# A fused attention and MLP kernel on one Trainium2 core: one front for two passes, two scales for w_in, and a new order of its tasks

## The chip, the core and the metric

The kernel runs on one NeuronCore of a Trainium2 chip. Five engines work side by side, each through its own list of instructions in a fixed order: TensorE (PE: matrix products and transposes), VectorE (DVE), ScalarE (ACT), GpSimd (POOL) and SyncE (SP), which starts the transfers between the chip's main memory (HBM) and the on-chip memory (SBUF). An engine waits where its next instruction needs a result that isn't there yet; it never takes a later one first. TensorE writes its products into a small memory of its own (PSUM), from where VectorE and ScalarE read them. The metric is the time of one execution in microseconds of the device.

## The reference

Attention for 8 batches of 8 heads, with 576 positions and 64 numbers a head, and then a two-layer MLP over all 4608 tokens. A position sees its own block of 64 and the blocks before it.

```python
scores = np.matmul(q, k.transpose(0, 1, 3, 2)) / np.sqrt(D)
scores = np.where(block_i >= block_j, scores, -1e9)      # blocks of 64 positions
attn = np.exp(scores - scores.max(-1, keepdims=True))
attn = attn / (attn.sum(-1, keepdims=True) + 1e-9)
o = np.matmul(attn, v)                                   # (8, 8, 576, 64)
x = o.transpose(0, 2, 1, 3).reshape(8 * 576, 512)
h = x @ w_in                                             # 512 -> 2048
out = np.square(np.maximum(h, 0.0)) @ w_out              # 2048 -> 512
```

## The kernel before

All numbers are fp32 in and out, but most products run on halves: a number is split into a high and a low f16 (`h`, then `l` from what the high half left over), and a product of two such numbers is three products, high by high, high by low and low by high. So that the halves use f16's range, each operand is first scaled by a power of two that is found from its largest value.

**Attention.** The work is cut into 40 passes, each for one batch and two heads. Passes 0 to 7 are short (the first 192 positions of batches 0 and 1), 8 to 11 do the rest of batch 0 in fp32 turns, and 12 to 39 are turned by DMA and need v in halves. A pass has these tasks, the letter being the name in the planner: `A` scores on TensorE (tile `side`), `B` their maxima on VectorE (`nmx`), `C` exponentials on ScalarE (`p`, with sums `sm`), `S` and `R` the reciprocals of the sums (`rs`), `D`, `H`, `L` the probabilities in halves (`p_rows`), `T` or `E` and `F` the transposition (`p_turned`), `G` the products with v (`px`), `X` their copy to `x`. A pass from 12 on also has a **front**, which finds v's scale: `fv` (ScalarE sums the absolute values of each row into `st`), `fa` (TensorE turns that column into a row, `pm`), `fb` (VectorE takes its largest, `top`), `fc` (TensorE spreads this over 128 partitions), `fd` (VectorE keeps the exponent, `m`), `fe` (three GpSimd steps: `m`, the scale `s`, and `xsc`), `vh` (high half of v, ScalarE) and `vl` (low half, VectorE).

**Norm.** For each of the 12 chunks of 384 tokens, `nq` adds up the squares `sq` of x on TensorE; VectorE makes a factor from it, and `h` and `l` write x in halves into `xt_all`.

**MLP.** The first four chunks are plain: for each of 16 units `ph{chunk}_{f}`, twelve products of 128x384 (`pair<-xt_all,w`), then `pos` and `sqr` (relu and square, tile `r`), `top` (the high half, a CAST into `hidden`) and `rem` (the low half, a subtraction `hidden<-r,hidden`). The other eight chunks save products in the manner of Strassen, with seven half-size products `p1` to `p7` for four units (tile `group`) and additions on ScalarE and VectorE. Behind both, `po` multiplies `hidden` with w_out (`pair<-w,hidden`), `ob` scales the result by the token's factor `uv` (one step on VectorE, two on ScalarE), and `out` stores it.

**Weights.** w_in and w_out come in 16 slices each. Before a slice can be used, its numbers are made whole (`bits` on GpSimd, `prelu` on ScalarE, `join` on VectorE), its largest value is found (`max`), and a chain `w0a` to `w0e` (w_in) or `w1a` to `w1e` (w_out) of VectorE and TensorE steps makes one scale out of all 16; then each slice is cast (`cast`) and its low half made (`low`).

**What sets the order.** A planner in the program (`Plan`) builds the lists of all engines ahead of time. `add(name, queue, ns, after, rank, make, takes, frees)` registers a task with its engine, or with a price for each of several engines, what it waits for, its rank and the buffers that it takes and gives back. `run` goes through an imagined time: it takes the task that can start earliest, among equals the one of the lowest rank, and puts it on the engine where it would end first. `DRAGS` says by what share of a GpSimd task's time VectorE is counted as held up. The ranks come from constants (`W0`, `W1`, `CHAIN`, `CALM`, `FRONT`, `TURN`) and from a table of single corrections, `SHIFTS`:

```python
if q == "POOL" and free["DVE"] > at:
    free["DVE"] += self.drag(name) * queues[q]
```

All instructions are recorded by one helper, so they all stand on one line of the program (L124); they are told apart by their tiles.

Of the kernel before, what the change touches and what calls it, by code (L numbers as in the profile page):

```python
# [19 lines left out]
P = 128  # L20
D = 64
# [12 lines left out]
CALM = 1195.46  # L34
# [19 lines left out]
W0 = (-248.45, 10.9, 139.39, 8.21, 175.27, 11.63, 23.26)  # L54
W1 = (-30.45, -241.86, -561.58, -723.11, -96.62)
NORMS = (-3.68, -3.62)
YR = (90.87, 1.94, 1.28, -9.6)
UR = (225.07, 13.43, 15.26)
LATER = 16
EASE = 61.67  # L60
SPARE = 157.67
SLACK = 0
EARLY = 542.67
BEGIN = 281.87
FILLER = 10000
CHAIN = 488.46
FRONT = 95.73
# [4 lines left out]
TURN = (2121.43, -14.33)  # L72
# [28 lines left out]
A20 32, A21 -9.5, A32 -520, A9 -300, B12 6.4, B14 520, B15 -190, B17 -8.6, B23 -97, B25 130, B27 74, B29 -220, B30 -51, B31 -120, B33 430,  # L101
B35 960, B37 -230, B38 -1100, B4 61, C12 730, C13 690, D6 1200, D7 640, D8 30, E4 870, F8 900, H12 -270, H16 270, H20 390, H21 210, H32 350,
H36 130, L13 76, L17 -240, L18 -440, L19 -780, L26 110, L28 -360, L33 -1500, L34 -590, Q6 740, R12 -930, R13 28, R20 -420, R3 -110, R38
-380, R5 -550, S12 -120, S8 -2200, T15 670, T18 72, T31 -190, X18 -450, X19 250, c226 150, fa12 620, fb12 -1200, fb14 21, fb21 -580, fd14
920, fd19 4.7, fv33 1000, h015 150, h1 98, h2 110, h234 200, h44 -11, h46 -490, h53 -1400, h54 -890, h65 1400, ic0 -460, ic1 -420, l014 51,
l2 290, l233 38, l42 540, l44 -2, l54 7.5, load21 -170, low0 -6, ob0 26, ob7 230, p1 -32, p23 -21, p36 -130, p38 -160, p410 -63, p45 -180,
p47 200, p48 -190, p510 -13, p610 -140, p63 -250, p65 -120, p77 290, p78 -91, po7 1300, pos0 -88, pos1 -820, pos2 420, prelu0 -51, r10 -340,
r11 -190, rem0 -4.5, rem116 -160, rem123 580, rem218 4.2, s15 240, s16 -710, s23 20, s24 84, s26 -58, s32 610, s35 -4.6, sa0 58, sa2 128.6,
sq116 110, sq123 -160, sq126 -130, sq128 210, sq2110 -280, sq223 390, sqr0 1600, t0 240, top1 1200, top4 -390, uv0 -98, vl17 820, vl21 -38,
vl31 110, vl32 710, vl34 -21, vl36 -21  # L110
# [40 lines left out]

class Plan:


    DRAGS = (("bits", 0.4), ("cast", 0.3), ("rem", 0.15), ("D", 0.35), ("top", 0), ("t", 0.4), ("s", 0.2))
    LAG = {"PE": 250, "DVE": 180, "ACT": 220, "POOL": 200, "SP": 100}

    def __init__(self, rings):
        self.tasks, self.rings, self.holders, self.before, self.lands = {}, rings, {}, {}, {}
# [15 lines left out]
    def run(self):  # L175
# [12 lines left out]
        def ready(name):  # L188
# [10 lines left out]
            for q in queues:  # L199
                lag = self.LAG[q] + (MARGIN if q == "PE" and rank >= LATE else 0)  # L200
                at = free[q]
                for n in needs:
                    at = max(at, issued[n] if on[n] == q and n not in self.lands else end[n] + lag)
                cost = at + queues[q] + (EASE + (SPARE if name[0] in "Dc" and "POOL" in queues else 0) if q == "DVE" else 0)
                if best is None or cost < best[0]:
                    best = cost, at, q
            yield best[1], rank, name, best[2]

        while open_:
# [27 lines left out]
            if len(queues) > 1:  # L237
                make(q)
            else:
                make()  # L240
        assert not any(need.values()), [n for n in need if need[n]][:20]
# [3 lines left out]
def attention_moe_kernel(ctx: ExitStack, tc: tile.TileContext, qk1, v1, qk, ks, vm, vt, w_in, w_out, out):  # L245
# [35 lines left out]
    vraw = [const.tile([P, 2, 5, D], F32, name=f"vraw{i}") for i in range(2)]  # L281

# [57 lines left out]
    tokA = const.tile([P, 1], F32, name="tokA")  # L340
    tokB = const.tile([P, 1], F32, name="tokB")
# [62 lines left out]
    wsc = [const.tile([P, 1], F32, name=f"wsc{i}") for i in range(2)]  # L404
# [15 lines left out]
    beyond = []  # L420

# [6 lines left out]
    def weight_scale(wi, m):  # L428

        tok = (tokA, tokB)[wi]  # L430
        if wi:
            nc.vector.tensor_scalar(tok, m, 2.0**-5, None, op0=ALU.mult)
        else:
# [3 lines left out]
        nc.vector.tensor_scalar(  # L437
            wsc[wi].bitcast(I32), tok.bitcast(I32), -1, 254 << 23, op0=ALU.mult, op1=ALU.add
        )
        if wi:  # L440
            nc.vector.tensor_scalar(tokB, tokB, tokA, None, op0=ALU.mult)
        else:
            nc.vector.tensor_scalar(tokA, tokA, 2.0 ** (A_X + A_W - 1), None, op0=ALU.mult)

    def weight_part(wi, f):
# [20 lines left out]
        def summed(o):  # L466
            nc.scalar.activation(raws[wi][f][2], whole, AF.Prelu, scale=2.0**-9, alpha=-1.0, accum_out=o)

        def high(q):
            if q == "ACT":  # L470
                nc.scalar.activation(wh, whole, AF.Copy, scale=wsc[wi])
            else:
                (nc.vector if q == "DVE" else nc.gpsimd).tensor_scalar(wh, whole, wsc[wi], None, op0=ALU.mult)

        def low():
            nc.vector.scalar_tensor_tensor(wl, whole, wsc[wi], wh, op0=ALU.mult, op1=ALU.subtract)
# [45 lines left out]
    def front(t):  # L522


        u, c = t["u"], t["chunks"]
        v32 = t["v32"][:, :, 0:c, :]
        box = {}

        def v_sum():
            box["st"] = small.tile([P, 1], F32, tag="st", name=f"st_{u}")  # L530
            t["v16"] = p2.tile([P, 2, 2, 5, D], F16, tag="v16", name=f"v16_{u}")
            nc.scalar.activation(t["v16"][:, 0, :, 0:c, :], v32, AF.Abs, accum_out=box["st"])

        def turned():
            pm = box["pm"] = ps_x.tile([P, 512], F32, tag="x", name=f"pm_{u}")
            nc.tensor.transpose(pm[:1, :P], box["st"], ident)

        def largest():
            box["top"] = small.tile([1, 1], BF16, tag="top", name=f"top_{u}", bufs=1)
# [1238 lines left out]
```

## Time and profile before

| what | value |
|---|---|
| median of three runs | 989.27 us (988.4 to 989.52) |
| profiled execution | 989.28 us |
| its span in the trace | 987.5 us |
| TensorE busy | 956.1 us of the span (97%), 8027 products |
| VectorE busy | 786.2 us (80%) |
| ScalarE busy | 606.0 us (61%) |
| GpSimd busy | 210.0 us (21%) |

The span goes from the first to the last instruction that the trace holds; what the execution took beyond it lies around it. Busy time counts an engine's own instructions, and a matrix product that runs at half clock counts for as long as it lasts. A row of the timeline groups neighbouring instructions of one kind (x12 is twelve of them), and the bracket at its end is the idle time ahead of it with what ended it: `[1.39 <-DMA first<-in_qk]` is 1.39 us of waiting for a transfer into the tile `first`. In a row of groups the last column is all idle time ahead of the group's instructions, with the releaser of most of it.

### The profile page before, as it was taken

How to read it: one execution, taken by the hardware profiler on the slowest of the kernel's cores; microseconds unless marked ns; L12 is line 12 of the kernel's file. 1: busy time of each engine (PE TensorE's matmuls, PEld its weight loads, DVE VectorE, ACT ScalarE, POOL GpSimd, SP SyncE). 2: the span in 40 equal slices, each digit the busy share in tenths (PEclk: the TensorE clock that was granted, in tenths of full speed). 3: DMA queues.
4: the chain of work that ended last, by engine and by line, in shares of the span. 5: the costliest groups of instructions: out<-in, count | busy, mean ns of one | idle time of the engine just before them, and what ended most of it. 6: DMA issues, size and time to landing. Idle time of an engine off the chain costs nothing.

```text
span 987.5 us, 20889 instructions
## 1 busy us (share of the span) xinstructions
PE 956.1 (97%) x8027; PEld 598.8 (61%) x8027; DVE 786.2 (80%) x1749; ACT 606.0 (61%) x1535; POOL 210.0 (21%) x354
## 2 busy tenths in 40 slices
PE   6789899999999999999999999999999999999998
PEld 5455544554554554596486586596577476496675
DVE  6798998878999669799789698899679788576361
ACT  5799963865887685565465566667566567353240
POOL 3635310002334213132022012122012011101000
PEclk9889989999999999999999999999999999999999
DMA  9835454585753713954760652945561560700001
GB/s 357 308 136 179 116 157 88 127 177 135 153 135 94 153 35 67 206 110 93 148 142 12 133 122 45 211 68 150 132 143 21 136 127 20 137 12 11 23 2 33
DMA packets 221649, 114.92 MB, mean 116 GB/s; under 512 B 195290, under 2 KB 203756, under 8 KB 221548
## 3 DMA queue, kind: packets, MB, share of 16 engines
q1 hardware_dynamic: 221548, 113.57, 48.2%
q8 instruction: 63, 1.03, 0.4%
q14 instruction: 38, 0.31, 0.1%
HBM read 58.21 MB, written 9.46 MB: 69 GB/s over the span
## 4 chain that ended last, share of the span: by engine, by line
PE 68%; DVE 13%; ACT 7%; issue 6%; DMA 3%; POOL 2%; SPq 0%; POOLq 0%; DVEq 0%; ACTq 0%
PE pair L124 33%; PE group L124 21%; PE side L124 6%; PE px L124 5%; DVE w L124 3%; DVE p_rows L124 3%; ACT p L124 2%; DVE nmx L124 2%; PE po L124 2%; ACT r L124 1%; DMA w<-in_w_in 1%; DVE _AluOpType.subtract L124 1%; DVE xt_all L124 1%; DMA hidden<-in_w_in 1%; DVE r L124 1%
## 5 line engine op out<-in xcount | busy, mean ns | idle before, releaser
L124 PE MATMUL pair<-w,hidden 128*128 128x512 f16 (+1 forms) x1680 | 380.2, 376 | 2.1 <-DVE ob L124 1.4
L124 PEld LDWEIGHTS <-hidden 128*128 128x128 f16 x1776 | 167.4, 98 | 185.3 <-issue 14.8
L124 PEld LDWEIGHTS <-w 128*128 128x128 f16 x2304 | 202.2, 98 | 71.6 <-issue 20.7
L124 ACT ACTIVATE p<-side,nmx 128x576 f32<-128x576 f32 (+8 forms) x264 | 139.7, 539 | 87.3 <-DVE nmx L124 73.1
L124 PE MATMUL group<-xt_all,w 128*128 128x192 f16 x1536 | 141.8, 246 | 0.0
L124 DVE SCALAR_TENSOR_TENSOR p_rows<-p,rs,p_rows 128x64 f16<-128x64 f32 (+6 forms) x264 | 138.2, 562 | 4.5 <-DMA p_turned<-p_rows 1.5
L124 PE MATMUL pair<-xt_all,w 128*128 128x384 f16 x768 | 136.3, 334 | 3.4 <-DVE xt_all L124 3.4
L124 DVE TENSOR_REDUCE nmx<-side 128x1 f32<-128x448 f32 (+8 forms) x288 | 123.2, 479 | 12.8 <-PE side L124 12.5
L124 ACT CAST hidden<-r 128x384 f16<-128x384 f32 x188 | 94.8, 510 | 26.4 <-DVE r L124 23.5
L124 POOL TENSOR_SCALAR sm<-sm 128x2 f32<-128x2 f32 (+2 forms) x104 | 29.1, 279 | 381.5 <-ACT p L124 373.3
L124 PE MATMUL group<-xt_all,turned_w 128*128 128x192 f16 x1152 | 108.6, 246 | 0.0
L124 PE MATMUL side<-qk 64*64 64x512 f32 (+2 forms) x480 | 95.2, 492 | 6.7 <-ACT p L124 6.1
L124 ACT ACTIVATE r<-group 128x384 f32<-128x384 f32 x100 | 48.9, 489 | 85.0 <-PE group L124 83.8
L124 PEld LDWEIGHTS <-turned_w 128*128 128x128 f16 x1152 | 95.8, 98 | 7.5 <-issue 2.0
L124 POOL TENSOR_TENSOR hidden<-r,hidden 128x384 f16<-128x384 f32 x55 | 57.9, 1053 | 195.6 <-ACT hidden L124 131.0
L124 DVE TENSOR_TENSOR hidden<-r,hidden 128x384 f16<-128x384 f32 x137 | 81.3, 599 | 16.3 <-ACT hidden L124 15.1
L124 ACT ACTIVATE p_rows<-p,rs 128x128 f16<-128x128 f32 (+9 forms) x148 | 67.6, 501 | 37.8 <-DVE rs L124 34.3
L124 PE MATMUL side<-ks,qk 64*64 64x128 f32 (+4 forms) x576 | 90.6, 420 | 0.0
L124 PE MATMUL px<-p_turned,v 128*64 128x384 f16 (+5 forms) x1168 | 70.9, 270 | 0.5 <-ACT x L124 0.2
L124 PEld LDWEIGHTS <-v 128*64 128x64 f16 x1128 | 50.6, 110 | 27.4 <-issue 16.9
L124 DVE SCALAR_TENSOR_TENSOR r<-group,r 128x384 f32<-128x384 f32 x96 | 52.9, 552 | 14.0 <-PE group L124 10.3
L124 DVE SCALAR_TENSOR_TENSOR r<-r 128x384 f32<-128x384 f32 x98 | 58.8, 603 | 3.6 <-ACT r L124 1.2
(147 smaller groups left out, 1069.3 us busy)
## 6 DMA issues: line engine op xcount, KB each, us to landing
qk<-in_qk SPq DMA_DIRECT2D x32, 576.0 KB
ks<-in_ks SPq DMA_DIRECT2D x32, 320.0 KB
vraw<-in_vm SPq DMA_DIRECT2D x30, 256.0 KB
w<-in_w_out SPq DMA_DIRECT2D x10, 512.0 KB
out<-ob SPq DMA_DIRECT2D x17, 256.0 KB
w<-in_w_in SPq DMA_DIRECT2D x8, 512.0 KB
out<-ob SPq DMA_DIRECT2D x26, 128.0 KB
hidden<-in_w_in SPq DMA_DIRECT2D x6, 512.0 KB
```

The lines of the kernel that those rows point to most:

```text
L124: i = make(*a, **k)
```

## The change

It has three parts.

- **w_in gets two scales**, one for slices 0 to 7 and one for 8 to 15 (`SHARES`). The chain `w0a` to `w0e` becomes two chains (`w0a0` to `w0e0`, `w0a1` to `w0e1`) and a step `w0e` that joins them; the casts of the first eight slices wait for the first chain alone. What was a constant factor (`C_H`) in the steps behind w_in's products becomes a pointer to `rescale`, with a value for each half.
- **A front is done for two passes at once.** The values of v are loaded for both (`vals{i}`, apart from the rows of q and k), `fv` writes two columns of `st`, and `fa` to `fe` run once for both, on two columns. The high half `vh` may go to VectorE, and only it takes a buffer `v16`; `fv` writes its unused result to `unread`.
- **The planner** gets other numbers in `DRAGS`, a table `BIAS` that is added to the price of a kind of task on an engine, more tasks that may go to VectorE (`F`, `X`, `Q`, w_out's `max`), and new constants and `SHIFTS` throughout.

```diff
-    DRAGS = (("bits", 0.4), ("cast", 0.3), ("rem", 0.15), ("D", 0.35), ("top", 0), ("t", 0.4), ("s", 0.2))
+    DRAGS = (("bits", 0.3), ("cast", 0.2), ("rem", 0.42), ("D", 0.25), ("top", 0), ("t", 0.5), ("s", 0.55), ("fe", 0.05))
...
+SHARES = (8, 16)
...
+BIAS = {'D ACT': 677, 'D DVE': -122, 'D POOL': 142, 'F ACT': -1214, 'F DVE': -817, 'H ACT': -44, 'H DVE': -119, 'c ACT': -342, 'c DVE': -40, 'cast ACT': 2073, 'cast DVE': -672, 'cast POOL': 818, 'h ACT': -137, 'h DVE': -231, 'ob ACT': -14706, 'ob DVE': 211, 'rem DVE': 0, 'rem POOL': -5929, 's DVE': 590, 's POOL': 360, 'sq ACT': 728, 'sq DVE': 1129, 't DVE': -13772, 't POOL': 722, 'top ACT': 157, 'top DVE': 249, 'X DVE': 3195, 'Q DVE': -81, 'max DVE': 88, 'vh ACT': 5746, 'Q ACT': -26, 'X ACT': 444, 'max ACT': -1113, 'pos ACT': 179, 'pos DVE': 13, 'vh DVE': -436}
...
-                cost = at + queues[q] + (EASE + (SPARE if name[0] in "Dc" and "POOL" in queues else 0) if q == "DVE" else 0)
+                cost = at + queues[q] + BIAS.get(f"{kind_of(name)} {q}", 0) + (EASE + (SPARE if name[0] in "Dc" and "POOL" in queues else 0) if q == "DVE" else 0)
...
+    def shares_joined():
+
+        nc.vector.reduce_max(tokA, toks, axis=AX.X)
+        nc.vector.tensor_scalar(rescale[:, 0:1].bitcast(I32), tokA.bitcast(I32), -1, 254 << 23, op0=ALU.mult, op1=ALU.add)
+        nc.vector.tensor_scalar(rescale, toks, rescale[:, 0:1], C_H, op0=ALU.mult, op1=ALU.mult)
+        nc.vector.tensor_scalar(tokA, tokA, 2.0 ** (A_X + A_W - 1), None, op0=ALU.mult)
...
-        def v_sum():
-            box["st"] = small.tile([P, 1], F32, tag="st", name=f"st_{u}")
-            t["v16"] = p2.tile([P, 2, 2, 5, D], F16, tag="v16", name=f"v16_{u}")
-            nc.scalar.activation(t["v16"][:, 0, :, 0:c, :], v32, AF.Abs, accum_out=box["st"])
+        def v_sum(e):
+            t = pair[e]
+            if e == 0:
+                box["st"] = small.tile([P, 2], F32, tag="st", name=f"st_{u}")
+            c = t["chunks"]
+            nc.scalar.activation(unread[:, :, 0:c, :], t["v32"][:, :, 0:c, :], AF.Abs, accum_out=box["st"][:, e : e + 1])
 
         def turned():
             pm = box["pm"] = ps_x.tile([P, 512], F32, tag="x", name=f"pm_{u}")
-            nc.tensor.transpose(pm[:1, :P], box["st"], ident)
+            nc.tensor.transpose(pm[:2, :P], box["st"], ident)
 
         def largest():
-            box["top"] = small.tile([1, 1], BF16, tag="top", name=f"top_{u}", bufs=1)
-            nc.vector.tensor_reduce(box["top"], box["pm"][:1, :P], axis=AX.X, op=ALU.max)
+            mx = small.tile([2, 1], F32, tag="top", name=f"mx_{u}", bufs=1)
+            dg = box["dg"] = small.tile([2, 2], BF16, tag="vd", name=f"vd_{u}", bufs=1)
+            nc.vector.tensor_reduce(mx, box["pm"][:2, :P], axis=AX.X, op=ALU.max)
+            nc.vector.tensor_scalar(dg, ident[:2, :2], mx, None, op0=ALU.mult)
 
         def spread():
-            nc.tensor.matmul(box["pm"][:, P : P + 1], ones_bf[:1], box["top"], start=True, stop=True)
+            nc.tensor.matmul(box["pm"][:, P : P + 2], ones_bf[:2], box["dg"], start=True, stop=True)
...
+            if i % 2 == 0:
...
+                if i - 2 >= WHOLE:
+                    prior = [f"vl{i - 2}", f"vl{i - 1}"]
...
+                add(f"vals{i}", "SP", 1900, prior, ahead + 1, both, size=2 * P * 2 * S * 4)
+                for e in range(2):
+                    add(f"fv{i + e}", "ACT", 740, [f"vals{i}"] + [f"fv{i}"] * e, r, go("v_sum", e))
+                add(f"fa{i}", "PE", 120, [f"fv{i}", f"fv{i + 1}"], r, go("turned"), ("x",))
```

The order of the instructions changes on every engine. The first place is TensorE's list at the end of chunk 0, before the change: here `nq` stands behind chunk 0's sixteenth unit, whose last product is the first row. (`_0_3` in a name is pass 12 and `_1_3` pass 13; the last number of a name is its buffer.)

```order
LDWEIGHTS w_104
MATMUL pair_81<-xt_all,w_104 128x384
LDWEIGHTS ones_bf
MATMUL nq_1_1414<-sq_1_0_1149,ones_bf 128x384
LDWEIGHTS ones_bf
MATMUL nq_1_1414<-sq_1_2_1361,ones_bf 128x384
MATMUL pm_1_3_1417<-ident,st_1_3_1386 1x128
MATMUL side_75<-qk_1_3_1008 64x512 x2
...
MATMUL pm_0_3_1441<-top_0_3_1453,ones_bf 128x1
LDWEIGHTS w_104
MATMUL pair_76<-xt_all,w_104 128x384
```

The last row is chunk 1's first product; between `nq` and it there are two transposes of fronts, four groups of scores and one spread. After the change the same stretch reads:

```order
MATMUL nq_1_1374<-sq_1_2_1320,ones_bf 128x384
MATMUL pm_0_3_1377<-ident,st_0_3_1339 2x128
LDWEIGHTS w_105
MATMUL pair_81<-xt_all,w_105 128x384
...
MATMUL side_80<-qk_1_3_956 64x320 x2
MATMUL side_80<-ks_1_3_958,qk_1_3_956 64x256 x2
MATMUL side_75<-qk_1_3_956 64x512 x2
MATMUL side_75<-ks_1_3_958,qk_1_3_956 64x384 x2
...
MATMUL pm_0_3_1377<-vd_0_3_1448,ones_bf 128x2
LDWEIGHTS w_105
MATMUL pair_76<-xt_all,w_105 128x384
```

Now `nq` stands behind the thirteenth unit: the fourteenth unit (twelve products) lies between it and the scores, and the fifteenth and sixteenth (24 products, at the second "...") between the scores and the spread. The fronts of passes 12 and 13 (`_0_3` and `_1_3`) are one transpose of two columns.

The second place is GpSimd's list where the second layer's input of chunk 1 is made, before the change. `sm` are sums of exponentials, `m`, `s` and `xsc` a front.

```order
TENSOR_SCALAR sm_1_3_7_1646<-sm_1_3_7_1646 128x2
TENSOR_SCALAR sm_1_3_4_1825<-sm_1_3_4_1825 128x2
TENSOR_TENSOR hidden<-r_0_1515,hidden 128x384
TENSOR_SCALAR m_2_3_1890<-m_2_3_1890 128x1
TENSOR_SCALAR s_2_3_1900<-m_2_3_1890 128x1
TENSOR_SCALAR xsc_2_3_1902<-m_2_3_1890 128x1
TENSOR_SCALAR sm_2_3_8_1893<-sm_2_3_8_1893 128x2
```

One low half of `hidden` stands between sums and fronts. After the change:

```order
TENSOR_SCALAR sm_1_3_7_1810<-sm_1_3_7_1810 128x2
TENSOR_TENSOR hidden<-r_0_1533,hidden 128x384
TENSOR_TENSOR hidden<-r_1_1554,hidden 128x384
TENSOR_SCALAR sm_1_3_4_1839<-sm_1_3_4_1839 128x2
TENSOR_TENSOR hidden<-r_2_1581,hidden 128x384
TENSOR_TENSOR hidden<-r_3_1631,hidden 128x384
TENSOR_TENSOR hidden<-r_4_1661,hidden 128x384
TENSOR_SCALAR sm_2_3_8_1888<-sm_2_3_8_1888 128x2
TENSOR_SCALAR sm_2_3_7_1931<-sm_2_3_7_1931 128x2
TENSOR_TENSOR hidden<-r_5_1996,hidden 128x384
TENSOR_SCALAR m_2_3_2034<-m_2_3_2034 128x2
```

Six subtractions stand there now, and a sum of exponentials has up to three of them ahead of it. Over the whole program GpSimd's low halves go from 55 to 176 and VectorE's from 137 to 16; `ob` goes from 29 on VectorE and 8 on ScalarE to all 37 on ScalarE; 27 of 28 `vh` move from ScalarE to VectorE, and 19 steps of the turned weights from GpSimd to VectorE.

## Rows read from the trace of the kernel before

**Rows 1.** The page: span, then busy time of TensorE and three engines.
```profile
span 987.5 us, 20889 instructions
...
PE 956.1 (97%) x8027; PEld 598.8 (61%) x8027; DVE 786.2 (80%) x1749; ACT 606.0 (61%) x1535; POOL 210.0 (21%) x354
```

**Rows 2.** Windows: length, busy PE, PEld, DVE, ACT, POOL, granted clock, DMA share, GB/s.
```profile
0.00:56.00 56.00, 38.47 (x313) 26.65 (x314) 41.32 (x113) 37.99 (x114) 26.63 (x53) 0.87 0.90 331
56.00:118.00 62.00, 60.73 (x438) 34.84 (x437) 58.04 (x120) 59.53 (x154) 27.83 (x36) 0.98 0.40 128
118.00:125.00 7.00, 2.83 (x22) 0.88 (x21) 6.86 (x13) 6.84 (x18) 2.06 (x3) 0.92 0.63 143
125.00:140.00 15.00, 15.00 (x100) 8.29 (x102) 13.05 (x33) 12.75 (x30) 4.47 (x9) 0.81 0.71 219
140.00:985.00 845.00, 839.02 (x7166) 528.13 (x7156) 666.90 (x1474) 488.91 (x1223) 149.01 (x254) 1.00 0.46 99
```

**Rows 3.** Timeline of TensorE around 26 and 55 us: start, length, idle before.
```profile
26.08 1.54 PE L124 MATMUL side<-first 64*64 64x192 f32 x12 [1.39 <-DMA first<-in_qk]
...
54.26 0.49 PE L124 MATMUL pair<-xt_all,w 128*128 128x384 f16 x1
55.98 3.41 PE L124 MATMUL pair<-xt_all,w 128*128 128x384 f16 x11 [1.23 <-DVE xt_all L124]
```

**Rows 4.** Timeline of ScalarE ahead of the first unit.
```profile
51.59 1.41 ACT L124 ACTIVATE p_rows<-p,rs 128x576 f32<-128x576 f32 x2
...
53.37 0.83 ACT L124 CAST xt_all<-x 128x768 f16<-128x768 f32 x1
```

**Rows 5.** Timeline of TensorE from 117 to 136 us.
```profile
117.52 0.49 PE L124 MATMUL nq<-sq,ones_bf 128*128 128x384 bf16 x2
...
123.00 0.32 PE L124 MATMUL pair<-xt_all,w 128*128 128x384 f16 x1 [0.71 <-DVE xt_all L124]
124.80 8.72 PE L124 MATMUL pair<-xt_all,w 128*128 128x384 f16 x35 [1.47 <-DVE xt_all L124]
133.45 0.17 PE L124 MATMUL pm<-top,ones_bf 1*128 1x1 bf16 x1
133.56 2.12 PE L124 MATMUL pair<-xt_all,w 128*128 128x384 f16 x12
```

**Rows 6.** Timeline of VectorE: w_out's scale and its first slice.
```profile
132.76 0.17 DVE L124 TENSOR_REDUCE st<-stw 128x1 f32<-128x16 f32 x1 [0.68 <-ACT raw L124]
...
139.34 0.75 DVE L124 SCALAR_TENSOR_TENSOR w<-w,wsc 128x512 f16<-128x512 f32 x1
```

**Rows 7.** Timeline of TensorE: a front's transpose and what follows it.
```profile
177.69 0.27 PE L124 MATMUL pm<-ident,st 128*1 128x128 f32 x1
177.89 0.49 PE L124 MATMUL side<-qk 64*64 64x320 f32 x2
```

**Rows 8.** Groups of like instructions: count, busy us, mean ns, idle before.
```profile
L124 DVE TENSOR_TENSOR hidden<-r,hidden 128x384 f16<-128x384 f32 x137 | 81.3, 599 | 16.3 <-ACT hidden L124 15.1
...
L124 POOL TENSOR_TENSOR hidden<-r,hidden 128x384 f16<-128x384 f32 x55 | 57.9, 1053 | 195.6 <-ACT hidden L124 131.0 <-PE group L124 64.0
...
L124 DVE TENSOR_SCALAR ob<-pair,uv 128x512 f32<-128x512 f32 x26 | 21.0, 806 | 35.2 <-PE pair L124 35.1
...
L124 ACT ACTIVATE ob<-ob,uv 128x512 f32<-128x512 f32 x8 | 5.8, 722 | 0.3
L124 ACT ACTIVATE ob<-pair,uv 128x512 f32<-128x512 f32 x8 | 5.5, 685 | 7.8 <-PE pair L124 7.7
```

**Rows 9.** Timeline of GpSimd at 431 us.
```profile
430.79 2.10 POOL L124 TENSOR_TENSOR hidden<-r,hidden 128x384 f16<-128x384 f32 x2
```

**Rows 10.** Timeline of VectorE from 432 us.
```profile
432.12 1.19 DVE L124 TENSOR_TENSOR hidden<-r,hidden 128x384 f16<-128x384 f32 x1
...
433.67 0.55 DVE L124 TENSOR_TENSOR hidden<-r,hidden 128x384 f16<-128x384 f32 x1
```

**Rows 11.** Timeline of the end.
```profile
984.27 0.54 DVE L124 TENSOR_SCALAR ob<-po,uv 128x256 f32<-128x256 f32 x1 [4.70 <-PE po L124]
```

More of the change, by code (lines that the diff above doesn't have):

```diff
@@ L33 @@
 ALONE = 14
-CALM = 1195.46
+SHARES = (8, 16)
+CALM = 213.05
 A_ATT = 14
@@ L105 @@
[L105 to L108, printed above, removed]
@@ L240, in run @@
                 make()
+            rest = self.within.get(name)
+            if rest and q == "DVE":
+                open_.remove(rest)
+                on[rest], end[rest], issued[rest] = q, end[name], issued[name]
+                for u in users.get(rest, ()):
+                    need[u] -= 1
+                    if not need[u]:
+                        open_.add(u)
         assert not any(need.values()), [n for n in need if need[n]][:20]
@@ L1673, in plan_all @@
-            box = {}
-            def start(t=t, box=box):
-                box.update(front(t))
-            def go(name, first=False, box=box, start=start):
-                def run():
-                    if first:
-                        start()
-                    box[name]()
-                return run
-            r = front_rank
-            add(f"fv{i}", "ACT", 740, [f"load{i}"], r, go("v_sum", True), ("v16",))
-            add(f"fa{i}", "PE", 120, [f"fv{i}"], r, go("turned"), ("x",))
@@ L1689, in plan_all @@
-            add(f"fb{i}", "DVE", 210, [f"fa{i}"], r, go("largest"), ("top",))
-            add(f"fc{i}", "PE", 100, [f"fb{i}"], r, go("spread"), frees=[(f"fb{i}", "top")])
-            add(f"fd{i}", "DVE", 130, [f"fc{i}"], r, go("read"), frees=[(f"fa{i}", "x")])
-            add(f"fe{i}", "POOL", 1020, [f"fd{i}"], r, go("scales"))
+            last = [f"load{i - 1}"] if i > 8 else []
+            ahead = order.get(f"Y{i - 8}", 56 + 3 * (i - 8) if early else base - 150)
+            add(
+                f"load{i}", "SP", 900, last, ahead, lambda t=t: load_rows(t), ("qk", "ks"), size=P * (3 * S + D) * 4,
+            )
@@ new lines, in plan_all, with go, run, both @@
+            pair = passes[i : i + 2]
+            if i % 2 == 0:
+                box = {}
+                def go(name, *e, pair=pair, box=box):
+                    def run(*q):
+                        if not box:
+                            box.update(front(pair))
+                        box[name](*e, *q)
+                    return run
+                def both(pair=pair):
+                    for t in pair:
+                        load_values(t)
+                if i - 2 >= WHOLE:
+                    prior = [f"vl{i - 2}", f"vl{i - 1}"]
+                elif i > 11:
+                    prior = [f"G{i - 4}_1", f"G{i - 3}_1"]
+                else:
+                    prior = [f"G{q}" for q in range(4)]
+                r = front_rank
+                add(f"vals{i}", "SP", 1900, prior, ahead + 1, both, size=2 * P * 2 * S * 4)
+                for e in range(2):
+                    add(f"fv{i + e}", "ACT", 740, [f"vals{i}"] + [f"fv{i}"] * e, r, go("v_sum", e))
+                add(f"fa{i}", "PE", 120, [f"fv{i}", f"fv{i + 1}"], r, go("turned"), ("x",))
+                add(f"fb{i}", "DVE", 320, [f"fa{i}"], r, go("largest"), ("top",))
+                add(f"fc{i}", "PE", 100, [f"fb{i}"], r, go("spread"), frees=[(f"fb{i}", "top")])
+                add(f"fd{i}", "DVE", 90, [f"fc{i}"], r, go("read"), frees=[(f"fa{i}", "x")])
+                add(f"fe{i}", "POOL", 1020, [f"fd{i}"], r, go("scales"))
```

246 lines of the change are left out of this document (152 added, 94 removed).

## The prediction

> **What bounds the kernel now.** I read the page first: TensorE is busy 956.1 of 987.5 us, VectorE 80%, ScalarE 61%, GpSimd 21% [rows 1]. That is a mean over stages that differ, so I read windows next [rows 2]. From 140 us to the end TensorE works 839.02 of 845 us at full clock: there the time is TensorE's own work, and all waits together are 6 us. From 56 to 118 us three engines are full at once (TensorE 60.73, ScalarE 59.53, VectorE 58.04 of 62). What is lost lies in three places: TensorE works only 38.47 of the first 56 us, 2.83 of the 7 us from 118, and from 125 to 140 its mean granted clock is 0.81. The profiled execution took 989.28 us, its span 987.5 and 1.78 around it; the median of the three runs is 989.27, so the sum is made against 989.3.
>
> Two timelines show what these losses are. The first unit of chunk 0 (`ph0_0`, twelve products `pair<-xt_all,w`) has its first product at 54.26 and waits 1.23 us for VectorE's low halves; it goes on at 55.98 [rows 3]. ScalarE's cast of the high halves stands at 53.37, right behind a queue of other work [rows 4]. The second loss comes after chunk 0's sixteenth unit: the sums of squares `nq` run at 117.52, and until VectorE has normed chunk 1 from them TensorE has only a few scores and fronts. It gets the first product of chunk 1 at 123.00 and the rest at 124.80. Those 35 products then take 8.72 us, where 12 at the full rate take 2.12, so 35 would take 6.2: the half clock that follows the pause costs another 2.5 us [rows 5].
>
> **The change part by part.**
>
> *One front for two passes.* 28 fronts become 14, so 14 transposes and 14 one-column products leave TensorE, 13 pairs of them behind chunk 0. A transpose starts at 177.69 and its successor at 177.89, 0.20 us [rows 7]; a spread at 133.45 and its successor at 133.56, 0.11 us [rows 5]. 13 pairs at 0.31 are 4.0 us; since TensorE is full there, I book all of it. The bounds are 2.9 (both at 0.11) and 5.2 (both at 0.20). The other three engines lose work too (14 times each step on VectorE and GpSimd), all beside TensorE. What may be late: both values loads of a pair now wait until the pair before is split, and the fronts stand closer ahead of their products (by the count of products between them down to 5 to 8 us of TensorE for passes 26, 28, 30, 36 and 38). The list before has two as close (passes 30 and 38), in a stage that shows no wait of note. I take nothing for it, and 1 us for each of the five as the other end.
>
> *A scale for each half of w_in.* One more chain of five small VectorE steps and two products; the join adds four more, nine steps or 1.5 us of VectorE at 0.17 for a small one [rows 6], of which the gate of w_out's first slice sees all. The first half's casts need 8 slices instead of 16. Nothing waited for them alone: the gate of `ph0_0` was chunk 0's low halves [rows 3]. A pointer in place of a constant for the scale I cost at nothing, since VectorE's `ob` already takes pointers.
>
> *Order up to the first unit.* Ahead of the cast of rows 4 ScalarE's list is shorter by four writes of probabilities, two exponentials, one conversion and one copy. At 0.7 us for one (two took 1.41 [rows 4]) this is 5.6 at most; I take 5, so the cast stands at 48.4. But two transposes in front of `ph0_0` now need four of those writes, at the same 0.7, and a copy, some 3.1 us behind the cast's end, and the transposes themselves about 0.7: the unit runs from about 53 instead of 55.98, 3 us earlier. Passes 6 and 7 are loaded two slices earlier, which takes up to the 1.39 us that TensorE waited for this load [rows 3]; it is inside the 3.
>
> *Order around chunk 1's norm.* `nq` now stands behind the thirteenth unit, so three units, 6.4 us by 2.12 each, lie between it and chunk 1. That covers the 4.2 us of idling (7.00 less 2.83) [rows 2]. If the clock then stays up, another 2.5 [rows 5].
>
> *What caps both.* The product with w_out (`po0`) can't start before w_out's scale: its chain begins at 132.76 when ScalarE has reduced the sixteenth slice, and the first slice is ready 139.34 + 0.75 [rows 6]. ScalarE's list ahead of that reduction is as long as before; only idle time can leave it, of which it has 18.0 us up to 56 and 2.5 up to 118 [rows 2]. VectorE's list up to the first slice is some 4 us shorter. So of 3 + 4.2 + 2.5 us on TensorE, I take 5 us for the start of `po0`, less about 1 us for a group of scores that is moved behind it: 4 us. The bounds are 0 (ScalarE keeps all its idling) and 9.7.
>
> *More on GpSimd, all of `ob` on ScalarE.* 121 subtractions of `hidden` move from VectorE to GpSimd, where one takes 1053 instead of 599 ns; 29 `ob` move to ScalarE, 685 + 722 instead of 806 ns [rows 8]; 19 steps of the turned weights go back to VectorE. VectorE loses 121 times 0.6 = 73 us of work. What it gets back is contention: at 432.12 a subtraction of VectorE beside two of GpSimd took 1.19 us, the next 0.55 [rows 9, 10]. At 0.64 for each of 121 it would be 77 us, at nothing 0. The median row lies near the lower end (mean 599 against the 0.55 of a free one, with GpSimd at work 21% of the span), so VectorE ends with less to do than now. On TensorE's path I book nothing: what stands behind a longer subtraction on GpSimd is the next sum of exponentials and the next subtraction, and `po` waits for these; the cover is the other chunk's work which the list puts between. If that cover is gone each costs TensorE up to 0.45 us.
>
> Here a rule speaks against the change. The Trainium skill ("SBUF — State Buffer", Who interferes with whom) says that GpSimd shares a port pair with VectorE, and that the one which comes second is blocked for the whole instruction. The 1.19 us row agrees. By that rule each of the 121 could hold VectorE for its whole 1053 ns, 127 us, and VectorE would end busier than now; the rival of a late VectorE or GpSimd below is what would follow.
>
> *The end.* The last `ob` moves from VectorE, 0.54 us [rows 11], to two steps on ScalarE. At half of 685 + 722 and up to 0.9 us for both this adds 0.2 to 0.4; I take 0.3.
>
> Sum: 989.3 - 4.0 - 4.0 + 0.3 = 981.6, said as 981.5.
>
> **The rivals.**
>
> *Only the fronts count.* ScalarE's work ahead of w_out's scale (37.99 + 59.53 + 6.84 us by 125 [rows 2]) is the real gate and `po0` stays behind 139.34 + 0.75 or a microsecond earlier; the pause at 118 us turns into one ahead of `po0`. For it: ScalarE's 59.53 of 62. Against it: its 18 us of idling before. 989.3 - 4.0 + 0.3 = 985.6.
>
> *The pause goes with its half clock, and ScalarE keeps up.* 9.7 - 1 = 8.7 early, and the upper bound of the fronts: 989.3 - 8.7 - 5.2 + 0.3 = 975.7.
>
> *Late halves of `hidden`: slower.* In 32 groups of units GpSimd takes about four subtractions in a row. Four at 1.05 instead of 0.6 end 1.8 us later, and `po` of that slice, next in TensorE's order, waits. The gain of 7.7 is used up once TensorE waits 0.24 us in each group; at 0.5 us, 16 us, the time is 981.6 + 16 = 997.6. For it: TensorE's order is fixed when the kernel is built, so nothing fills such a wait, and rows 9 show two in a row on GpSimd already. Against it: GpSimd works 149.01 of 845 us [rows 2], and with 55 such subtractions the waits are 6 us in all.
>
> *No change.* Some of the late-subtraction case, 0.24 us a group, meets the gain: 989.
>
> **How the numbers follow.** The forecast has 0.47 (978 to 985), only the fronts 0.18, the full early gain 0.14, slower 0.13, no change 0.08. Within 0.2% means 987.3 to 991.3, about what three runs of this kernel can tell from no change. Faster is 0.47 + 0.18 + 0.14 = 0.79, same 0.08, slower 0.13. The range leaves out the slow case and the far part of the full early gain: 974.5 to 990.
>
> **What would show it.** Right: the window 118 to 125 has TensorE full, `ph1_0` starts by 119, `po0` by 136, 28 rows of `pm` products instead of 56, and from `po0` to the end some 4 us less than now with waits of 6 us or fewer. Wrong: a new wait of TensorE ahead of `po0` for VectorE's first slice of w_out (only the fronts), or waits of `pair<-w,hidden` for GpSimd's `hidden` spread over the stage after 400 us (slower). A half clock anywhere behind 60 us would cost half of its length.

## The result and the profile after

The changed kernel takes 978.53 us (median of 4 runs, 978.28 to 979.07) against 989.15 (4 runs in the same comparison): 0.9894 of the time, 95% interval 0.9882 to 0.9906. 981.5 us was forecast, with 7.8 us of gain; 10.6 came. The page and the windows of the profiled execution (979.07 us, 1.77 of it around the span), as in [rows 1, 2]:

```profile
span 977.3 us, 20978 instructions
...
PE 949.8 (97%) x8001; PEld 597.0 (61%) x8001; DVE 746.2 (76%) x1606; ACT 651.0 (67%) x1602; POOL 302.6 (31%) x419
```

```profile
0.00:56.00 56.00, 42.98 (x335) 29.68 (x336) 41.03 (x118) 39.12 (x118) 32.92 (x57) 0.82 0.84 315
56.00:118.00 62.00, 56.45 (x411) 30.77 (x410) 59.57 (x120) 60.96 (x152) 22.86 (x36) 0.97 0.49 143
118.00:125.00 7.00, 6.26 (x39) 3.59 (x38) 6.94 (x15) 6.94 (x18) 2.88 (x5) 1.00 0.83 211
125.00:140.00 15.00, 14.68 (x101) 8.18 (x101) 14.44 (x32) 13.40 (x31) 1.18 (x2) 1.00 0.65 176
```

TensorE fills 6.26 of the 7 us from 118, where it filled 2.83, and the half clock behind is gone. In return it works 4.3 us less between 56 and 118. Fixed windows mix two shifts; cut at what the kernel does, the account closes. These windows of both kernels go from chunk 1's first product to the product with w_out (`po0`), from there to TensorE's last product, and to the end (length, then busy PE, PEld, DVE, ACT, POOL, granted clock, DMA share, GB/s). Before:

```profile
123.00:140.75 17.75, 16.27 (x105) 8.53 (x105) 15.73 (x37) 15.40 (x35) 4.57 (x9) 0.81 0.73 223
140.75:984.23 843.48, 838.27 (x7158) 528.08 (x7154) 665.68 (x1471) 488.19 (x1222) 149.01 (x254) 1.00 0.46 99
984.23:987.50 3.27, 0.00 (x1) 0.00 (x0) 0.54 (x1) 0.00 (x0) 0.00 (x0) 0.99 0.12 40
```

After:

```profile
122.76:135.48 12.72, 12.28 (x93) 7.32 (x93) 12.38 (x31) 12.50 (x29) 3.18 (x5) 1.00 0.95 249
135.48:973.45 837.97, 833.86 (x7142) 526.86 (x7139) 628.49 (x1333) 532.70 (x1293) 242.75 (x321) 1.00 0.47 100
973.45:977.30 3.85, 0.10 (x1) 0.00 (x0) 0.00 (x0) 0.98 (x2) 0.00 (x0) 0.84 0.11 35
```

`po0` starts 5.27 us earlier; from there to the last product it takes 5.51 less, although a group of scores (1.0 us) has moved behind that start; the end is 0.58 longer. 5.27 + 5.51 - 0.58 = 10.20, the difference of the spans.

The timeline of TensorE between, after the change (start, length, idle before), answers to [rows 3, 5]:

```profile
52.03 2.11 PE L126 MATMUL pair<-xt_all,w 128*128 128x384 f16 x12
...
93.20 2.49 PE L126 MATMUL px<-p_turned,v 128*64 128x384 f32 x20 [1.86 <-ACT p_turned L126]
...
97.74 1.05 PE L126 MATMUL pt<-ident,p_rows 128*128 128x128 f32 x5 [0.46 <-ACT p_turned L126]
99.57 1.01 PE L126 MATMUL pt<-ident,p_rows 128*128 128x128 f32 x7 [0.78 <-ACT p_turned L126]
101.64 0.90 PE L126 MATMUL pt<-ident,p_rows 128*128 128x128 f32 x5 [1.06 <-ACT p_turned L126]
102.50 3.65 PE L126 MATMUL pair<-xt_all,w 128*128 128x384 f16 x12
...
113.95 0.49 PE L126 MATMUL nq<-sq,ones_bf 128*128 128x384 bf16 x2
...
118.66 4.06 PE L126 MATMUL pair<-xt_all,w 128*128 128x384 f16 x24 [0.61 <-ACT r L126]
...
122.76 2.12 PE L126 MATMUL pair<-xt_all,w 128*128 128x384 f16 x12
...
135.48 14.87 PE L126 MATMUL pair<-w,hidden 128*128 128x512 f16 x67
```

The first unit is over at 54.14, where it was over at 59.39: 5.25 us ahead. It starts 2.23 earlier, waits 1.23 less on the way, and works 1.79 us less, since before it ran mostly at half clock (granted clock 0.54 from 54.26 to 59.39). ScalarE's cast, which stood at 53.37 [rows 4], comes 6.7 us earlier:

```profile
46.65 0.86 ACT L126 CAST xt_all<-x 128x768 f16<-128x768 f32 x1
```

From the end of that unit to `po0` both kernels take the same time, 81.34 us against 81.36: the lead at `po0` is the lead of the first unit and no more. The pause at the norm and the half clock behind it are gone, but new losses stand against them, above all four waits for ScalarE's copies of `p_turned` between 91 and 102 us (4.16 together) and a unit at half clock behind them (3.65 instead of 2.11). By chunk 1's first product only 0.24 of the lead is left. But `nq` has run with three units still to come, so nothing waits for the norm, and from chunk 1's first product to `po0` it takes 12.72 us instead of 17.75.

The lead is no accident of one pair of profiles: in the eight of the changed order whose lists are the same up to `po0`, or nearly so, `po0` starts between 134.25 and 136.47 (mean 135.27), in the four of the order of before between 140.38 and 140.75.

The groups that the planner moved, as in [rows 8]:

```profile
L126 POOL TENSOR_TENSOR hidden<-r,hidden 128x384 f16<-128x384 f32 x176 | 180.8, 1036 | 222.0 <-ACT hidden L126 205.9 <-issue 7.8 <-DVE hidden L126 6.2
...
L126 ACT ACTIVATE ob<-ob,uv 128x512 f32<-128x512 f32 x35 | 25.3, 722 | 1.1
L126 ACT ACTIVATE ob<-pair,uv 128x512 f32<-128x512 f32 x34 | 23.3, 686 | 58.4 <-PE pair L126 58.1
```

### The profile page after: what moved, and what is told of

Read it like the earlier page. It is cut to its first block, busy times and chain, and to the rows that moved or that the text cites. A ratio compares the mean times of both kernels' runs of the same rounds, so it can differ in the third digit from the quotient of the medians.

```text
span 977.3 us, 20978 instructions
## 1 busy us (share of the span) xinstructions
PE 949.8 (97%) x8001; PEld 597.0 (61%) x8001; DVE 746.2 (76%) x1606; ACT 651.0 (67%) x1602; POOL 302.6 (31%) x419
## 4 chain that ended last, share of the span: by engine, by line
PE 80%; DVE 5%; ACT 5%; DMA 2%; issue 1%; SPq 0%; POOL 0%; POOLq 0%; ACTq 0%; DVEq 0%
PE pair L126 41%; PE group L126 23%; PE side L126 7%; PE px L126 6%; DVE w L126 2%; PE po L126 2%; DMA p_turned<-p_rows 1%; ACT wt L126 1%; DVE _AluOpType.subtract L126 1%; DVE p_rows L126 1%; ACT p L126 1%; ACT w L126 1%; ACT r L126 1%; ACT p_turned L126 0%; DVE nmx L126 0%
## 5 line engine op out<-in xcount | busy, mean ns | idle before, releaser
L126 POOL TENSOR_TENSOR hidden<-r,hidden 128x384 f16<-128x384 f32 x176 | 180.8, 1036 | 222.0 <-ACT hidden L126 205.9
L126 ACT ACTIVATE p<-side,nmx 128x256 f32<-128x256 f32 (+8 forms) x264 | 139.6, 538 | 71.3 <-DVE nmx L126 58.7
L126 DVE TENSOR_REDUCE nmx<-side 128x1 f32<-128x192 f32 (+8 forms) x288 | 123.7, 482 | 27.4 <-PE side L126 25.7
L126 DVE SCALAR_TENSOR_TENSOR p_rows<-p,rs,p_rows 128x64 f16<-128x64 f32 (+7 forms) x264 | 138.8, 568 | 5.6 <-DMA p_turned<-p_rows 3.3
L126 PE MATMUL pair<-xt_all,w 128*128 128x384 f16 x768 | 133.1, 329 | 0.8 <-ACT r L126 0.8
L126 DVE SCALAR_TENSOR_TENSOR r<-group,rescale,r 128x384 f32<-128x384 f32 x96 | 58.8, 613 | 76.6 <-PE group L126 46.0
L126 ACT ACTIVATE r<-group,rescale 128x384 f32<-128x384 f32 x118 | 67.7, 577 | 34.9 <-PE group L126 33.2
L126 ACT ACTIVATE p_rows<-p,rs 128x64 f16<-128x64 f32 (+11 forms) x151 | 68.0, 498 | 25.9 <-DVE rs L126 16.3
L126 ACT ACTIVATE r<-r 128x384 f32<-128x384 f32 x125 | 65.0, 523 | 5.1 <-DVE r L126 2.4
L126 DVE TENSOR_SCALAR p_rows<-p,rs 128x576 f16<-128x576 f32 (+9 forms) x135 | 63.6, 496 | 3.7 <-DMA p_turned<-p_rows 1.3
```

Of the source, the lines that this page charges most:

```text
L126: i = make(*a, **k)
```

## The experiments

In all but the first run on the scales the order is the finished list of tasks of one kernel, and the planner decides nothing anew: a variant changes an engine, a place in the list, or the products inside a task. Times are medians of 4 to 11 runs; the changed kernel's 978.53 (978.28 to 979.07) and the 989.2 to 989.4 of the kernel before are what they stand against.

**What a front costs TensorE.** First each small product stood twice:

```diff
-            nc.tensor.transpose(pm[:2, :P], box["st"], ident)
+            for _ in range(2):
+                nc.tensor.transpose(pm[:2, :P], box["st"], ident)
...
```

> The changed kernel, with each front's transpose and each spread issued twice on TensorE (14 more of each, 13 of each behind the start of the product with w_out); nothing else differs. Theory: TensorE is full there and a pair of such products costs it 0.31 us, so 13 pairs cost 4.0 us: 982.5 us; since the second one stands next to its like, 0.22 us a pair, 2.9 us in all, is the lower end: 981.4. Rival (the gain behind the start of the product with w_out came from waits, and the small products run in pauses): 0 to 0.5 us, 978.5 to 979.

980.22 us (979.31 to 980.79), 1.7 more: below the lower end. A second transpose behind the first took 0.11 us, but of two neighbouring spreads the first took 0.04 and the second 0.09, where a single one takes 0.10; and the product ahead of a spread, which is stretched by 0.10, is stretched once for both. So the extra products were put where the second front of a pair had stood, between two units (the two side by side, where those of a second front stood apart):

```diff
...
+                out += [(f"db{i}", "PE"), (f"da{i}", "PE")]     # one more spread, one more transpose
...
```

> The changed kernel with one more transpose and one more spread for each of the 13 pairs of fronts behind the start of the product with w_out, put one unit behind the pair's own transpose, so that they interrupt the products as the second front of a pair did before. Theory (such a pair costs TensorE 0.11 + 0.10 for itself and 0.10 by which it stretches the product ahead): 13 times 0.31 or 4.0 us, 982.5 us; the stretch from the start of the product with w_out to TensorE's end grows by 3.5 to 4.5 us. Rival (the run with the doubled neighbours had the true price, 0.13 us a pair): 1.7 us, 980.2 us.

983.83 us (982.84 to 984.16), 5.3 more. From `po0` to the last product in its profile (columns as above):

```profile
135.18:978.32 843.14, 838.16 (x7168) 528.62 (x7165) 627.26 (x1333) 533.40 (x1293) 244.60 (x321) 1.00 0.47 100
```

TensorE is busy 4.3 us longer there than in the changed kernel, 0.33 for each of 13 pairs, and waits 0.87 longer. The price that the prediction gave to a pair stands, and the cheap neighbour is the artefact.

**Are the three units what opens the gate?**

```diff
+UNITS = ["ph0_13", "pos0_12", "ph0_14", "pos0_13", "ph0_15"]
...
+    at = rest.index(("nq0_1", "PE"))
+    return rest[:at] + [(n, on[n]) for n in UNITS] + rest[at:]
```

> The changed kernel, with the fourteenth to sixteenth unit of chunk 0 (and two relus) put back ahead of the sums of squares, so that nothing lies between these and chunk 1; all other lists as they are. Theory: the pause returns; TensorE idles 5 to 7 us ahead of chunk 1's first unit, and products behind it run at half clock for 2 to 3 us more: the product with w_out starts 6 to 9 us later, 985 to 988 us. Rival (the scale of w_out sets that start, whatever TensorE does before): the pause moves and the start stays within 1.5 us: 978.5 to 980.

984.18 us (982.33 to 985.48), 5.7 more. TensorE in its profile:

```profile
120.36 0.49 PE L126 MATMUL nq<-sq,ones_bf 128*128 128x384 bf16 x2
...
126.63 0.16 PE L126 MATMUL pm<-vd,ones_bf 2*128 2x2 bf16 x1 [4.13 <-DVE vd L126]
127.01 0.48 PE L126 MATMUL pair<-xt_all,w 128*128 128x384 f16 x1 [0.22 <-ACT r L126]
128.28 8.39 PE L126 MATMUL pair<-xt_all,w 128*128 128x384 f16 x35 [0.79 <-DVE xt_all L126]
...
142.57 0.59 PE L126 MATMUL pair<-w,hidden 128*128 128x512 f16 x2
```

The pause is back with 5.14 us and the half clock with 8.39 for 35 products, almost as in [rows 5]; `po0` starts 7.09 later in this execution, the slowest of the five (985.48). The median is a little below the range named, the mechanism is the theory's. The rival, that the pause would only be moved, falls.

**The half clock alone.** In the kernel before, 32 small products of ones filled the pause:

```diff
+            if t["i"] == 12:
+                spin(pm[:, 2 * P :], 4)
...
+            if t["i"] == 12:
+                spin(box["pm"][:, 2 * P :], 10)
             nc.tensor.matmul(box["pm"][:, P : P + 1], ones_bf[:1], box["top"], start=True, stop=True)
+            if t["i"] == 12:
+                spin(box["pm"][:, 2 * P :], 18)
```

> The kernel before with 32 small products of ones (3.4 us at full rate) put into TensorE's pause between the sums of squares of chunk 1 and its first unit, so that the clock has no pause to fall in; they write to unused columns of a front's bank. Theory (the half clock behind the pause costs 2.5 us, and ScalarE, which waited 0.92 and 0.86 us for TensorE there, follows): the granted clock from 125 to 140 us is 1.0, and the time is 986.7 to 988. Rival (the scale of w_out holds the start): at most 0.7 us is gained, 988.5 or more.

990.11 us (988.34 to 992.78, eleven runs) against 989.39: nothing gained. Windows, then TensorE and VectorE around the stage:

```profile
125.00:140.00 15.00, 14.59 (x122) 9.08 (x119) 13.90 (x35) 13.31 (x31) 4.18 (x9) 1.00 0.75 239
```

```profile
126.62 6.01 PE L124 MATMUL pair<-xt_all,w 128*128 128x384 f16 x36
...
140.38 0.82 PE L124 MATMUL pair<-w,hidden 128*128 128x512 f16 x3
```

```profile
124.20 1.76 DVE L124 TENSOR_TENSOR xt_all<-x,xt_all 128x1536 f16<-128x1536 f32 x1
...
139.54 0.75 DVE L124 SCALAR_TENSOR_TENSOR w<-w,wsc 128x512 f16<-128x512 f32 x1
```

The clock stays up, and 36 products take 6.01 us where 35 took 8.72: the price of 2.5 us is right for the profile that it was read from (in the run below with all `ob` on ScalarE, whose list is the same up to there, the 35 took 7.40). Yet `po0` starts only 0.37 us earlier, at 140.38. In part that is the run's own doing: `nq` stood 1.2 us later in this execution (118.72), and the norm was ready at 125.96 (124.20 + 1.76), while the filler held chunk 1 back to 126.62. In part it is w_out's scale: its first slice is ready at 140.29, nearly the same moment. TensorE doesn't wait for it right ahead of `po0`, so two limits meet there and the run doesn't part them. In the order of before, the first slice was ready at 140.09 [rows 6], 0.66 us ahead of `po0` at 140.75. Unless the chain of that scale came earlier too, no more than these 0.66 us were to be had. This is the rival's side, and the time agrees with it; a filler that ends with the norm was not run.

**Does ScalarE's list hold `po0` now?**

```diff
+LEFT_OUT = [f"max1_{f}" for f in range(1, 16, 2)]
```

> The changed kernel without the maxima of every second slice of w_out (its scale is found from 8 of 16 slices): ScalarE's list ahead of w_out's scale is 8 times 0.75, 6 us, shorter, and nothing else changes. Theory (ScalarE's list sets the start of the product with w_out, by the copies for which TensorE waits from 91 to 102 us and by the reduction of the last slice): that start comes 3 to 5 us earlier, 973.5 to 975.5 us. Rival (TensorE's own work is the bound up to there): at most 1 us, 977.5 or more.

978.25 us (976.42 to 980.02, the profiled execution being the slowest): no change that can be told. The same stretch of the changed kernel, then of this one, and its `po0`:

```profile
52.00:118.00 66.00, 60.45 (x441) 33.10 (x440) 62.68 (x128) 64.96 (x163) 24.62 (x38) 0.97 0.46 135
```

```profile
52.00:118.00 66.00, 60.20 (x450) 33.14 (x446) 62.64 (x129) 61.59 (x150) 24.46 (x38) 1.00 0.44 136
```

```profile
136.47 0.38 PE L126 MATMUL pair<-w,hidden 128*128 128x512 f16 x1
```

ScalarE has 3.4 us less to do in it and is idle for as much longer; TensorE idles 5.80 us against 5.55, and VectorE is as busy as it was. `po0` starts 0.99 later than in the changed kernel's profile, but its first unit had started 1.28 later (53.31). The theory falls: the waits for copies don't come from the length of ScalarE's list alone. The rival's time came, but its reason doesn't hold either. In this profile and in two below (low halves back on VectorE, the mixture) the unit behind those waits ran at full clock, so that TensorE had 1.1 to 1.5 us less to do; still, from the first unit's end to `po0` they took 81.05, 81.20 and 81.26 us, hardly less than the 81.34 of the changed kernel. VectorE, busy for 62.6 to 62.7 of the 66 us in all four, was not varied. That three engines, each nearly full, wait for each other in turn there is likely, but only argued.

W_out's first slice in the changed kernel, to which the part on the cap returns:

```profile
133.59 0.75 DVE L126 SCALAR_TENSOR_TENSOR w<-w,wsc 128x512 f16<-128x512 f32 x1
```

**Two scales for w_in.** One chain for all slices, with the planner run anew on it:

```diff
-        return next(i for i, e in enumerate(SHARES) if f < e)
+        return 1
...
```

> The changed kernel with one scale for all 16 slices of w_in in the same order of tasks: the first half's chain is left out, and the first cast waits for the chain of all slices. Theory (two scales cost and give nothing): 978.5 us within 0.5; the first unit starts within 0.5 us of 52.0. Rival (the early scale let the first unit start sooner): the first unit starts 2 to 3 us later, and the time is 980 to 981.5.

1029.13 us (1027.51 to 1029.75). The text says "in the same order"; that was wrong, and it is what the run shows. The planner read the new dependency, and with ranks found for another graph it put out a poor order. Its longest waits from 100 to 170 us (total, times, longest):

```profile
POOL sm L126 <- ACT p L126: 30.8, 9, 14.3
...
ACT unread L126 <- DMA vraw<-in_vt: 8.0, 1, 8.0
...
PE pm_w L126 <- DVE st L126: 6.9, 1, 6.9
```

With the list kept, and the first cast moved behind the one chain:

```diff
-        c = rescale[:, share_of(f) : share_of(f) + 1]
+        c = rescale[:, 1:2]
...
+    rest = [x for x in seq if x[0] not in ONE + ("cast0_0",)]
+    at = rest.index(("w0e1", "DVE")) + 1
+    return rest[:at] + [("cast0_0", "POOL")] + rest[at:]
```

> As the run with one scale, but with the plan made for two, so that the order of tasks stays that of the changed kernel: the first half's chain (nine steps of VectorE, two small products and a transposition) is left out, the first cast waits for the chain of all slices, and nothing else moves. Theory (two scales cost and give nothing by themselves; the 50 us were the new order): 978.5 us within 1, the first unit of chunk 0 within 1 us of 52.0. Rival (the early scale let the first unit start sooner): 2 to 3 us later, 980.5 to 981.5.

978.43 us (977.52 to 979.93), and the first unit comes no later (seven steps of VectorE are left out, not the nine that the text names):

```profile
50.88 2.11 PE L126 MATMUL pair<-xt_all,w 128*128 128x384 f16 x12
```

The two scales by themselves give nothing and cost nothing that can be told, as forecast.

**Low halves on GpSimd.** In the changed kernel 121 of them went back to VectorE, and in the kernel before the same 121 went to GpSimd (the edit of the first run; that of the second is its mirror image):

```diff
+    return [(n, "DVE" if n[:3] == "rem" and n[3:] not in ON_POOL else q) for n, q in seq]
```

> The changed kernel with 121 low halves of hidden back on VectorE, in the same places of the list, as the kernel before had them (55 stay on GpSimd). Theory (their engine is off TensorE's path either way): 978.5 us within 1. First rival (the relief of VectorE is what took waits from TensorE behind the start of the product with w_out): 1 to 3 us slower, with waits for scores' maxima or for psum banks. Second rival (subtractions on GpSimd are late or hold VectorE up): 1 us or more faster.

> The kernel before with the 121 low halves of hidden on GpSimd that the change moved there, in the order of the kernel before. Theory (the move is off TensorE's path by itself): 989.2 us within 1. Rival of the prediction (low halves late, 0.24 to 0.5 us in each of 32 groups, unless the order is made for it): 8 to 16 us slower, 997 to 1005.

The first takes 978.14 us (977.21 to 978.61), the same as the changed kernel; the second 992.51 (991.38 to 994.48), 3.1 slower than before. From `po0` to the last product, first the one, then the other:

```profile
135.85:972.21 836.36, 833.86 (x7142) 526.58 (x7139) 654.20 (x1454) 534.61 (x1293) 117.94 (x200) 1.00 0.47 101
```

```profile
140.60:987.09 846.49, 838.95 (x7158) 527.65 (x7154) 647.21 (x1350) 487.35 (x1222) 270.60 (x375) 1.00 0.46 99
```

VectorE's group of `hidden` in the changed kernel, then with the 121 back on it:

```profile
L126 DVE TENSOR_TENSOR hidden<-r,hidden 128x384 f16<-128x384 f32 x16 | 9.3, 597 | 0.2
```

```profile
L126 DVE TENSOR_TENSOR hidden<-r,hidden 128x384 f16<-128x384 f32 x137 | 77.4, 569 | 32.9 <-ACT hidden L126 31.9
```

TensorE's idle time from `po0` on (length less busy) is 2.50 in the first against 4.11 in the changed kernel, and 7.54 in the second against 5.21 before. The other profiles with the halves on GpSimd in the changed order idle 3.3 to 5.0 there, the mixture below 2.12. So the move makes 1.6 to 2.3 us of waits; it is no part of the gain, and the rival's price of it (7.7 us and more) was far too high. None of the waits is for a low half: in the second run, TensorE's longest total behind `po0` is for ScalarE's exponentials, more than the 2.0 us of before, and no wait for GpSimd is in the list:

```profile
PE side L124 <- ACT p L124: 3.3, 5, 1.4
PE pair L124 <- DVE ob L124: 1.9, 4, 0.9
```

**`ob` on ScalarE.** The same pair of runs: 29 back to VectorE in the changed kernel, all to ScalarE in the kernel before.

```diff
+    return [(n, "DVE" if n[:2] == "ob" and n not in ON_ACT else q) for n, q in seq]
...
```

> The changed kernel with the 29 results ob that the kernel before had on VectorE put back there, in the same places of the list. Theory: TensorE again waits for VectorE to empty a bank, 1.0 to 1.4 us as before the change, and the end behind the last product is 0.5 us shorter: 979.0 to 979.5 us. Rival (ob is off the path but for the end): 978.0.

> The kernel before with all 37 results ob on ScalarE, in the same places of the list. Theory: TensorE's 1.4 us of waits for VectorE's ob go, the end gets 0.5 us longer: 988.3 us. Rival (ScalarE comes late with scores or with chunks instead): 989.2 or more.

979.15 us (978.08 to 981.06), not to be told from 978.53; and 993.48 (992.21 to 993.91), 4.1 slower than before. Windows of the first run, from `po0` to the last product and behind it, then TensorE's waits in the second behind `po0`:

```profile
134.44:973.10 838.66, 834.59 (x7141) 526.74 (x7139) 647.42 (x1361) 497.11 (x1237) 242.54 (x321) 1.00 0.47 100
973.10:976.30 3.20, 0.03 (x1) 0.00 (x0) 0.54 (x1) 0.00 (x0) 0.00 (x0) 1.00 0.12 41
```

```profile
PE side L124 <- ACT p L124: 2.6, 4, 0.9
PE pair L124 <- ACT ob L124: 1.7, 3, 0.8
PE pm L124 <- ACT v L124: 1.5, 3, 0.7
```

Both theories fail, the first although its range holds the median. In the changed kernel VectorE's `ob` come in time (TensorE idles 4.07 us against 4.11), so the last one is all that differs, 3.20 instead of 3.85, as the rival had it; the four times scatter over 3 us, and the median can't show that. In the kernel before, the rival holds: the move trades waits for VectorE's `ob` for waits for ScalarE's, and adds new ones for the front's sums `v` behind them.

**A mixture.** 121 low halves and the very last `ob` on VectorE:

```diff
+        return "DVE" if n == "ob11_2" or n[:3] == "rem" and n[3:] not in ON_POOL else q
```

> The changed kernel with 121 low halves of hidden on VectorE and the very last result ob on VectorE. Theory (the halves on GpSimd made 1.6 us of waits behind the start of the product with w_out, and the last ob in one step ends 0.4 us sooner): 0.5 to 2 us below the changed kernel, 976.5 to 978. Rival (the waits are scatter of single executions): only the end, 978.1.

976.90 us (976.41 to 977.48), 0.9871 of the time before, interval 0.9858 to 0.9885. TensorE idles 2.12 us behind `po0`:

```profile
135.88:972.07 836.19, 834.07 (x7142) 526.76 (x7139) 654.90 (x1454) 534.29 (x1293) 117.47 (x200) 1.00 0.47 101
```

It is the fastest of all, 1.6 us below the changed kernel and inside the theory's range, though the intervals of the two ratios overlap.

## Why the prediction was right, point by point

The measured 978.53 us lies at the early edge of the forecast's 978 to 985, and about as far from the forecast of 981.5 (3.0) as from the full early gain (975.7, 2.8 away). The rival in which only the fronts count falls, since `po0` starts 5.27 us earlier.

**The fronts** (4.0, bounds 2.9 and 5.2): 4.3 of work, 5.3 with the waits that they bring. The sum was right, its two parts were not, and that they made up for each other was luck. Behind `po0` a transpose holds TensorE for 0.11 us; it took 0.20 only where scores followed it, and [rows 7] is such a place. A spread costs 0.10 itself, as in [rows 5], but it also stretches the product ahead of it by 0.10 (a `pair<-w,hidden` there holds TensorE for 0.31 instead of 0.22), and the rows that the prediction used don't hold that.

**Two scales** (nothing): nothing.

**The first unit 3 us earlier**: it ended 5.25 earlier. Its cause as forecast, ScalarE's cast no longer behind other work, is what the trace shows (46.65, forecast 48.4); 1.79 of the 5.25 is a half clock that the prediction had not counted. No run isolates the order ahead of this unit, though the lead at `po0` is its lead. The prediction also has no term for what was lost behind it, the four waits for copies and the unit at half clock. It was sought at the one place where before had a pause, not where three full engines would meet again.

**The pause at the norm, with its half clock** (4.2 and 2.5): right as to place and price; putting the units back costs 5.7 us of time and 7.1 of `po0`. As a gain it didn't come on top of the first unit's: it paid for the waits and the half clock between 91 and 106 us. That `ph1_0` would start by 119 was wrong: it starts at 122.76, since the three units are now spent ahead of it.

**The cap** (5 of 9.7, because of ScalarE's list): the number came close, 6.3 of earlier work at `po0` with the moved scores against 5 (5.27 against 4 without), but this was luck, for its reason doesn't hold after the change. In the kernel before, w_out's first slice did come close ahead of `po0` (0.66 us). In the changed kernel the first slice is ready at 134.34 (133.59 + 0.75), 1.1 us before it is used, and a shorter list of ScalarE moved nothing. What was lost went into the waits and the half clock between 91 and 106 us; why the stretch from the first unit to `po0` takes the same 81 us again stays open.

**GpSimd** (nothing on TensorE's path, 0 to 77 us of contention): behind `po0` VectorE is busy 25.7 us longer when it does the 121 itself (654.20 against 628.49), though these are 68 us of work (its group of `hidden` goes from 9.3 to 77.4 us). The other 42 us, 0.35 for each, are what they cost VectorE in lengthened neighbours from GpSimd (in the order of before, by the same reckoning, 0.44). That lies in the middle of the bounds, not near the lower end as I argued from a mean. The Trainium skill ("SBUF — State Buffer", Who interferes with whom), by which the engine that comes second is blocked for the whole instruction, would allow up to 127 us, if every one of the 121 met an instruction that it blocks. The runs show a third of that. On TensorE's path it was 1.6 us of waits, not nothing. The rival of late halves had the sign, but neither the size nor the way: no wait behind `po0` was for a low half.

**The end** (0.3): 0.58. The two steps of a half tile take 0.98 us together by busy time, against 0.54.

**Not in the sum**: 1.1 us less of waits behind `po0`, and 1.1 of TensorE's work there that the small products don't explain (5.4 less with the moved scores counted, 4.3 of them fronts). No run isolates it.

## What to carry to other kernels

Put a small product back where it interrupted the large ones before you judge its price: a transpose and a spread cost 0.13 us next to their like, between two units 0.33. Moves between engines have no price of their own: `ob` on ScalarE cost 4.1 us in one order and nothing that can be told in the other. Where an order comes from tuned numbers, change one thing in the finished list; a changed graph under the old numbers cost 50 us and said nothing on what was changed. When a pause goes, look whether what stood right behind it moves too, and measure from the same early landmark in both kernels: here the pause went, and the stretch in which it lay took as long as before.

## What was not expected of the chip

The clock fell after the same waits in one execution and not in another. With 1.86, 0.46, 0.78 and 1.06 us of idling before 102 us the changed kernel ran the next unit in 3.65 us and shows a granted clock of 0.97 from 52 to 118; the mixture, with 1.93, 0.45, 0.79 and 1.08 at the same places, shows 1.00:

```profile
103.09 2.11 PE L126 MATMUL pair<-xt_all,w 128*128 128x384 f16 x12
```

It was no gain: `po0` still came 81.26 us behind the first unit's end, against 81.34. In eight profiles whose lists are the same up to there, the first unit starts between 50.96 and 53.31 us, and `po0` moves with it. Differences of 1 to 2 us in one profile's early part are scatter; the medians, the windows behind `po0` and the stretch from the first unit to `po0` carry a verdict.
